# The third of the transposes that put kept V into PSUM goes between scaling and mask of the seventh head

## Chip, cores and metric

The kernel runs on one core of a Trainium2 chip. The metric is the device time of one execution in microseconds (us), the median of several runs. Lower is better.

## The reference, cut to what matters

A decode step for a batch of 4: an attention layer A, a gated layer B, then A and B again with the same weights and the same caches.

```python
W = min(4096, max(256, Sk // 4))                      # 2048 cached positions
k = jnp.repeat(k_cache[:, :, Sk - W:, :], rep, axis=1)   # 8 heads of K/V, 4 query heads each
v = jnp.repeat(v_cache[:, :, Sk - W:, :], rep, axis=1)
scores = jnp.einsum("bhqd,bhkd->bhqk", q, k) * (Dh ** -0.5)
o = jnp.einsum("bhqk,bhkd->bhqd", softmax(scores), v)
A = o.transpose(...).reshape(B, Sq, Hq * Dh) @ wo
B = (sigmoid(x @ w_gate) * (x @ w_up)) @ w_down
x = x + A(layernorm(x)); x = x + B(layernorm(x)); x = x + A(layernorm(x)); x = x + B(layernorm(x))
```

## The kernel before, in words

Attention runs over the 8 heads of K and V one after another, all 4 batches of a head at once. K of all heads stays in SBUF from the first attention to the second (slots 0 to 31 of the tile `arena`); V passes through the remaining slots and is read from memory again for the second attention, except for a few tiles that are kept.

A unit of the first attention (lines 1171 to 1198) is, for head h: transposes of K on VectorE (L854), scores on TensorE (L872, L883), maximum and its spreading on VectorE (L896 to L908), exponentials on ScalarE (L911), a turn of the probabilities (TensorE L924, ScalarE L926, VectorE L931), the sum (TensorE L950) and its reciprocal (VectorE L957), and P times V on TensorE (`pv_unit`, L973, 32 matmuls for each of the two batch pairs). Then come, in this order: the **scaling** of the result by the reciprocal on VectorE (operation `oe0.h`, L981), a small permutation on TensorE (`pm0.h`, L991, 4 matmuls), the **mask** on VectorE (`oq0.h`, L996), and the product with `wo` on TensorE (L1162, 16 matmuls).

Two tiles of V of the last head are kept without staying in their slots. The slots of the tile Y, which is V of head 7 and batch pair 0, are wanted for the weights of the gated layer in between. So Y is moved into PSUM banks 0 to 3 by four VectorE transposes of 128 by 512 words (`stash`, L578, operations `st0` to `st3`), and is moved back in the second attention (L593). Half of the tile Z (batch pair 1) goes into banks 4 and 5 in the same way (`stash_half`, L600, `so0` and `so1`) and comes back at L606.

What sets the order: `_Plan` records operations with their dependences, `_schedule` (L92) makes each engine's order from estimated durations, and `_assign_sync` turns dependences into semaphore waits. Each engine works in its order. The order of the transposes is written out by hand as extra dependences in `attn_first` (lines 1183 to 1195): `st0`, `st1`, scaling of head 6, mask of head 6, `st2`, `st3`, scaling of head 7, `so0`, mask of head 7, `so1`.

All loads go through SyncE's queue in a fixed order (L398). A load waits there until its place in SBUF is free. Around the change these are the places: the fourth piece of `w_gate` goes to the first half of Y (free after `st0`, `st1` and head 7's first P times V), the first piece of `w_up` goes to the second half of Y (free after `st2` and `st3` too), the second piece of `w_up` to Z (free after `so1`), the third and fourth to places that the first pieces of `w_gate` held. The pieces of `w_down` and of `wq` for the second attention follow in the same manner, each into a place that an earlier piece has left.

After `so1` stands the first reduction of the gated layer's layer norm (L745), then its sum on TensorE (L750), the subtraction (L753) and the matmuls with `w_gate` and `w_up` (L1341), one group of four for each piece.

Of the kernel before, what the change touches and what calls it, by code (L numbers as in the profile page):

```python
# [278 lines left out]
def build(nc, A_x, A_k, A_v, A_wq, A_wo, B_wg, B_wu, B_wd, out, cfg=None):  # L279
# [42 lines left out]
    with es:  # L322
# [60 lines left out]
        def tile_ap(s):  # L383
            return arena[:, s * SLOT:(s + 2) * SLOT]
# [4 lines left out]
        def c_dve(n, rate=None):  # L389
            return tm["dve_fix"] + n * (tm["dve_f32"] if rate is None else rate)  # L390
# [65 lines left out]
        def give(*halves):  # L456
            hfree.update(halves)
            fill()

        def need(name):  # L460
            while name not in where:
                take_load()
            return where[name]

        def done(name):
            left[name] -= 1
            if left[name] == 0:
                s = where.pop(name)
                if name in on_free:
                    on_free[name](s)  # L470
                else:
                    pool.release(s)
                fill()
# [99 lines left out]
        def stash(name, ns, after=()):  # L573
            s = need(name)
            for n in ns:
                b = STASH[n]
                src = tile_ap(s)[:, n * 1024:(n + 1) * 1024].bitcast(F32)
                o = P.op("vector", "st%d" % n, c_dve(512), lambda v, src=src, b=b: v.transpose(ps[:, b, :], src),  # L578
                         r=[("slot", s + n // 2)], w=[("stash", n)], banks=(b,), after=after)
            if n == len(STASH) - 1:  # L580
                done(name)
            return o

        def named(name):
            return [o for o in P.ops if o.name == name]
# [12 lines left out]
        def stash_half(n, after):  # L598
            src = slot_ap(base[Z])[:, n * 1024:(n + 1) * 1024].bitcast(F32)
            return P.op("vector", "so%d" % n, c_dve(512), lambda v: v.transpose(ps[:, OBS[n], :], src),  # L600
                        r=[("slot", base[Z])], w=[("so", n)], banks=(OBS[n],), after=after)
# [248 lines left out]
        def k_transpose(h):  # L850
            need(("K", h))
            for t in range(4):
                v32 = slot_ap(4 * h + t).bitcast(F32)
                P.op("vector", "T%d_%d" % (h, t), c_dve(1024), lambda v, v32=v32: v.transpose(v32, v32),  # L854
                     r=[("slot", 4 * h + t)], w=[("slot", 4 * h + t)])
# [66 lines left out]
        def turn_p(L, tag, k2, pb, wide=False):  # L922
            P.op("tensor", "pp" + tag, tm["pe_sq"],
                 lambda pe: pe.matmul(ps[:, pb, :], perm[:, :], prow[:, :], start=True, stop=True),  # L924
                 r=[("prow",)] + perms, w=[("ppb", pb)], banks=(pb,))
            P.op("scalar", "pc" + tag, c_act(512), lambda a: a.copy(prow[:, :], ps[:, pb, :]),  # L926
                 r=[("ppb", pb)], w=[("prow",)], banks=(pb,))
            et = ebuf[:, k2 * 256:(k2 + 1) * 256]
            if wide:
                et = et.rearrange("p (g m x) -> p m g x", g=4, m=8)  # L930
            P.op("vector", "pt" + tag, c_dve(256), lambda v: v.transpose(et, prow[:, :].bitcast(F32)),  # L931
                 r=[("prow",)], w=[("e", k2)])
            if L == 0:
                sums_old(tag, k2)
# [216 lines left out]
        def wo_unit(tag, h, ov, k2, first, final):  # L1151
            name = ("wo", h // 2)
            s = need(name)
            o = h % 2 * REP * D

            half = REP // 2 if tag == "0.%d" % (HKV - 1) else REP
            for r0 in range(0, REP, half):
                def e_wo(pe, r0=r0):
                    last = None
                    for r_ in range(r0, r0 + half):  # L1160
                        for c in range(NC):
                            last = pe.matmul(ps[:, WB, c * NR:(c + 1) * NR],  # L1162
                                             tile_ap(s)[:, o + r_ * D + c * 128:o + r_ * D + (c + 1) * 128],
                                             ov[:, r_ * NR:(r_ + 1) * NR], start=(first and r_ == 0 and c == 0),
                                             stop=(final and r_ == REP - 1), skip_group_check=True)
                    return last
                P.op("tensor", "WO%s_%d_%d" % (tag, h, r0), NC * half * tm["pe_pair"], e_wo,
                     r=[("half",) if r0 else ("slot", s + h % 2)] + [("op", k2)], w=[("psw",)], banks=(WB,))
            done(name)

        def attn_first():
            def front(h):
                k_transpose(h)
                softmax_unit("0.%d" % h, h)
                turn = lambda: turn_p(0, "0.%d" % h, h % 2, PBS[h % 2])
                return turn

            for h in range(2):
                front(h)()
            for h in range(HKV):  # L1180
                tag = "0.%d" % h
                turn = front(h + 2) if h + 2 < HKV else None
                if h == HKV - 1:
                    oe, oq = named("oe0.%d" % (h - 1)), named("oq0.%d" % (h - 1))
                    oe[0].deps.add(stash(stashed, (0, 1)))
                    st = stash(stashed, (2, 3), oq)
                    need(Z)
                op = pv_unit(tag, h, h % 2, v_tiles[(0, h)])
                if h == HKV - 1:
                    oe, oq = named("oe" + tag), named("oq" + tag)  # L1190
                    oe[0].deps.add(st)
                    oq[0].deps.add(stash_half(0, oe))
                    so = stash_half(1, oq)
                    give(base[Z])
                if turn is not None:
                    turn()
                wo_unit(tag, h, op, h % 2, False, h == HKV - 1)
            return so
# [226 lines left out]
        stashed = ("V",) + keep[0] + (0,)  # L1425
# [30 lines left out]
        x_in()  # L1456
        q_first(layer_norm("A", 0, NB, True))
        so = attn_first()
        n = len(P.ops)
        glu(0, 0, NB, (ps[:, WB, 0:REP * NX], [("psw",)], (WB,), lambda: attn_add(0)))  # L1460
# [75 lines left out]
```

## Time and profile before

| | |
|---|---|
| median of 3 runs | 179.22 us (178.72, 179.22, 180.37) |
| the profiled execution | 178.55 us, of which the span from first to last instruction is 176.8 us |
| TensorE busy | 105.5 us (60% of the span), 1653 matmuls |
| VectorE busy | 104.2 us (59%), 256 instructions |
| ScalarE, GpSimd busy | 32.7 us, 21.6 us |
| read from memory | 70.26 MB, 397 GB/s over the span |
| VectorE transposes L578 | 4 instructions, 684 to 728 ns each, from 99.3 us on |
| mean granted clock of TensorE | 0.949 |

Times in the views count from the first instruction. Busy time is the sum of an engine's instructions; "idle before" is the time for which an engine stood before an instruction, with what ended it behind the arrow. The chain of waits is followed back from the last instruction. A line with "x2" covers instructions that follow each other, from the start of the first to the end of the last. SPq is SyncE's queue, which issues the loads; the time to landing of a load runs from its issue to its semaphore.

### The profile page before, as it was taken

How to read it: one execution, taken by the hardware profiler on the slowest of the kernel's cores; microseconds unless marked ns; L12 is line 12 of the kernel's file. 1: busy time of each engine (PE TensorE's matmuls, PEld its weight loads, DVE VectorE, ACT ScalarE, POOL GpSimd, SP SyncE). 2: the span in 40 equal slices, each digit the busy share in tenths (PEclk: the TensorE clock that was granted, in tenths of full speed). 3: DMA queues.
4: the chain of work that ended last, by engine and by line, in shares of the span. 5: the costliest groups of instructions: out<-in, count | busy, mean ns of one | idle time of the engine just before them, and what ended most of it. 6: DMA issues, size and time to landing. Idle time of an engine off the chain costs nothing.

```text
span 176.8 us, 3904 instructions
## 1 busy us (share of the span) xinstructions
PE 105.5 (60%) x1653; PEld 54.7 (31%) x1653; DVE 104.2 (59%) x256; ACT 32.7 (18%) x87; POOL 21.6 (12%) x88
## 2 busy tenths in 40 slices
PE   0536346383852734707518967466877999776754
PEld 0202102241431431603404852052223444345412
DVE  6307997838477375594383582322299999752341
ACT  2002031312030210300301101000043455440011
POOL 6100010101010100100100100000011354342000
PEclk9999999999999999999999999999999999995555
DMA  5999999999999999999999999999999999999991
GB/s 183 426 428 424 423 423 417 411 426 419 417 413 421 423 419 421 411 424 424 411 417 432 400 402 392 406 405 382 410 398 406 423 423 419 419 417 407 405 388 39
DMA packets 12882, 70.52 MB, mean 399 GB/s; under 512 B 1336, under 2 KB 1344, under 8 KB 6720
## 3 DMA queue, kind: packets, MB, share of 16 engines
q1 hardware_dynamic: 12856, 70.26, 97.4%
q8 instruction: 13, 0.21, 0.5%
q14 instruction: 5, 0.04, 0.1%
q10 hardware_dynamic: 8, 0.00, 0.0%
HBM read 70.26 MB, written 0.00 MB: 397 GB/s over the span
## 4 chain that ended last, share of the span: by engine, by line
DMA 38%; DVE 32%; PE 19%; SPq 4%; issue 3%; ACT 2%; DVEq 0%; ACTq 0%
DMA arena<-in_B_w_down_dram 15%; DMA arena<-in_A_v_cache_dram 15%; DVE arena L854 11%; PE ps L883 7%; DVE nmax L896 5%; DMA arena<-in_B_w_gate_dram 4%; DMA arena<-in_A_wq_dram 4%; SPq L398 4%; PE ps L973 3%; PE ps L872 2%; DVE nmax L900 2%; DVE mxt L904 2%; DVE ebuf L931 2%; PE ps L924 2%; DVE arena L1064 2%
## 5 line engine op out<-in xcount | busy, mean ns | idle before, releaser
L854 DVE STREAM_TRANSPOSE arena<-arena 128x1024 f32<-128x1024 f32 x32 | 37.0, 1202 | 0.0
L883 PE MATMUL ps<-arena,qbd 128*32 128x512 bf16 x256 | 25.0, 525 | 0.1
L896 DVE TENSOR_REDUCE nmax<-ps 128x1 f32<-128x512 f32 x16 | 10.8, 676 | 19.6 <-PE ps L883 19.5
L872 PE MATMUL ps<-msk_m,msk_s 128*32 128x512 bf16 x64 | 8.4, 512 | 22.4 <-DVE arena L854 21.8
L973 PE MATMUL ps<-ebuf,arena 128*128 128x8 bf16 x576 | 17.8, 168 | 4.5 <-DMA arena<-in_A_v_cache_dram 4.3
L973 PEld LDWEIGHTS ps<-ebuf,arena 128*128 128x128 bf16 x576 | 16.8, 104 | 9.7 <-DMA arena<-in_A_v_cache_dram 5.3
L911 ACT ACTIVATE prow<-ps,nmax 128x512 bf16<-128x512 f32 x16 | 11.0, 687 | 35.2 <-DVE nmax L908 29.6
L847 ACT CAST qbd<-ps 128x256 bf16<-128x256 f32 x16 | 5.9, 370 | 44.9 <-PE ps L883 35.1
L924 PE MATMUL ps<-prow,perm 128*128 128x512 bf16 x16 | 7.9, 496 | 8.2 <-ACT prow L911 8.2
L940 POOL CAST s<-psm 128x1 bf16<-128x1 f32 x9 | 1.7, 187 | 83.9 <-ACT prow L911 83.9
L883 PEld LDWEIGHTS ps<-arena,qbd 128*32 128x32 bf16 x256 | 8.3, 119 | 10.0 <-issue 7.2
L795 PE MATMUL ps<-arena,xn 128*4 128x512 bf16 x64 | 8.3, 569 | 5.0 <-DMA arena<-in_A_wq_dram 4.7
L926 ACT CAST prow<-ps 128x512 bf16<-128x512 f32 x16 | 9.4, 585 | 9.9 <-PE ps L924 9.9
L1341 PE MATMUL ps<-arena,xn 128*4 128x448 bf16 x64 | 7.6, 550 | 3.8 <-DMA arena<-in_B_w_up_dram 2.1
L931 DVE STREAM_TRANSPOSE ebuf<-prow 128x256 f32<-128x256 f32 x16 | 7.0, 435 | 3.8 <-ACT prow L926 3.7
L872 PEld LDWEIGHTS ps<-msk_m,msk_s 128*32 128x32 bf16 x64 | 1.7, 97 | 24.1 <-DVE arena L854 22.7
L773 ACT ACTIVATE lnv<-ps 128x4 f32<-128x4 f32 x4 | 0.7, 173 | 41.1 <-PE ps L769 41.1
L807 DVE STREAM_TRANSPOSE ebuf<-ps 128x512 f32<-128x512 f32 x3 | 2.2, 717 | 10.2 <-PE ps L795 10.1
L842 PE MATMUL ps<-qh,eyew 32*128 32x64 bf16 x64 | 5.5, 215 | 3.3 <-ACT qbd L847 2.4
L1055 PE MATMUL ps<-arena,ebuf 128*32 128x512 bf16 x112 | 7.3, 381 | 0.2 <-DVE nmax L908 0.2
L1162 PE MATMUL ps<-onp,arena 128*128 128x16 bf16 x144 | 5.3, 175 | 2.9 <-DVE onp L996 2.6
L981 DVE TENSOR_TENSOR onb<-ps,rinv 128x16 bf16<-128x16 f32 x9 | 1.7, 185 | 8.3 <-PE ps L973 8.1
(112 smaller groups left out, 132.6 us busy)
## 6 DMA issues: line engine op xcount, KB each, us to landing
arena<-in_A_v_cache_dram SPq DMA_DIRECT2D x27, 1024.0 KB, 22.4
arena<-in_A_k_cache_dram SPq DMA_DIRECT2D x16, 1024.0 KB, 25.2
arena<-in_A_wq_dram SPq DMA_DIRECT2D x4, 1024.0 KB, 7.9
arena<-in_A_wq_dram SPq DMA_DIRECT2D x8, 512.0 KB, 6.2
arena<-in_A_wo_dram SPq DMA_DIRECT2D x3, 1024.0 KB, 26.2
arena<-in_B_w_down_dram SPq DMA_DIRECT2D x4, 512.0 KB, 6.3
arena<-in_B_w_gate_dram SPq DMA_DIRECT2D x4, 448.0 KB, 8.2
arena<-in_B_w_up_dram SPq DMA_DIRECT2D x4, 448.0 KB, 5.4
```

Source lines behind the costliest of these rows:

```text
L795: last = pe.matmul(ps[32 * hh:32 * hh + NB, qb, :], xn[:, c * NB:(c + 1) * NB], src[:, o + hh * 512:o + (hh + 1) * 512], start=(c == 0), s ...
L854: P.op("vector", "T%d_%d" % (h, t), c_dve(1024), lambda v, v32=v32: v.transpose(v32, v32), r=[("slot", 4 * h + t)], w=[("slot", 4 * h + t)])
L872: last = pe.matmul(ps[32 * gi:32 * gi + 32, bank, :], msk_s[:, :], msk_m[:, :].unsqueeze(1).broadcast_to([128, 256, 2]), start=True, stop= ...
L883: last = pe.matmul(ps[32 * gi:32 * gi + 32, bank, :], qbd[:, q0:q0 + 32], kt[:, cp // 2, cp % 2, jh * NJ:(jh + 1) * NJ, :], start=False, s ...
L896: lambda v: v.tensor_reduce(nmax[:, k2:k2 + 1], ps[:, bank, :], AXX, ALU.max),
L911: lambda a: a.activation(prow[:, :].rearrange("p (m x t) -> p m x t", x=32, t=2), ps[:, bank, :].rearrange("p (m t x) -> p m x t", x=32, t ...
L924: lambda pe: pe.matmul(ps[:, pb, :], perm[:, :], prow[:, :], start=True, stop=True),
L926: P.op("scalar", "pc" + tag, c_act(512), lambda a: a.copy(prow[:, :], ps[:, pb, :]), r=[("ppb", pb)], w=[("prow",)], banks=(pb,))
L931: P.op("vector", "pt" + tag, c_dve(256), lambda v: v.transpose(et, prow[:, :].bitcast(F32)), r=[("prow",)], w=[("e", k2)])
L973: last = pe.matmul(ps[:, ob, bp * 8:bp * 8 + 8], src[:, j * 128:(j + 1) * 128], ev[:, j % 2, j % 16 // 2, x0:x0 + 8], start=(j == 0), stop ...
L1055: last = pe.matmul(ps[32 * g:32 * g + 32, ob, :], ew[:, g, mq, t], src.rearrange("p (m t d) -> p t m d", t=2, d=128)[:, t], start=(n == 0) ...
L1341: last = pe.matmul(ps[32 * g:32 * g + NB, gub[n], 0:NF], xn[:, c * NB:(c + 1) * NB], slot_ap(s)[:, g * NF:(g + 1) * NF], start=(c == 0), s ...
```

## The change

`st2` and `st3` were recorded together, both after the mask of head 6 (`oq0.6`). Now `st2` depends on the scaling of head 6 (`oe0.6`), the mask depends on `st2`, and `st3` depends on the mask. VectorE's order becomes: `st0`, `st1`, scaling, `st2`, mask, `st3`, scaling of head 7. No instruction is added or removed, and the orders of TensorE, ScalarE, GpSimd and SyncE's queue are those of before. The mask waits for two semaphores now (VectorE's own, for `st2`, and TensorE's).

```diff
                 if h == HKV - 1:
                     oe, oq = named("oe0.%d" % (h - 1)), named("oq0.%d" % (h - 1))
                     oe[0].deps.add(stash(stashed, (0, 1)))
-                    st = stash(stashed, (2, 3), oq)
+                    oq[0].deps.add(stash(stashed, (2,), oe))
+                    st = stash(stashed, (3,), oq)
                     need(Z)
```

## Prediction

> **What bounds the kernel now.** I read the page first (engine shares, slices, queues), then the chain of waits from 97 us on, then VectorE's and TensorE's timelines around the transposes, then the loads' times to landing, and last the stretches of the gated layer.
>
> The page, slices and queues:
>
> ```profile
> span 176.8 us, 3904 instructions
> PEclk9999999999999999999999999999999999995555
> DMA  5999999999999999999999999999999999999991
> q1 hardware_dynamic: 12856, 70.26, 97.4%
> HBM read 70.26 MB, written 0.00 MB: 397 GB/s over the span
> ```
>
> No compute engine is above 60%, but the 16 DMA engines are 90% busy or more in every slice but the first and the last; queue 1 alone takes 97.4% of their time. Only a change that lets the stream of loads begin earlier, run dry less, or end with a shorter tail moves the end. The last load lands at 173.35 us (chain: 152.41 + 20.94), and the tail behind it takes 3.4 us.
>
> The chain of waits, its long pieces of the stretch after the change:
>
> ```profile
> 101.75 7.12 DMA arena<-in_B_w_gate_dram
> ...
> 110.89 6.29 DMA arena<-in_B_w_down_dram
> ...
> 117.85 6.48 DMA arena<-in_A_wq_dram
> ...
> 152.41 20.94 DMA arena<-in_B_w_down_dram
> ```
>
> From 101.75 us on the chain is a line of loads that stand in the queue behind other loads. 448 KB at 405 GB/s are 1.13 us of transfer, so most of the 7.12 us of the first is waiting for its turn.
>
> VectorE's timeline, start, length, instruction:
>
> ```profile
> 99.30 1.32 DVE L578 STREAM_TRANSPOSE ps<-arena 128x512 f32<-128x512 f32 x2
> 100.73 0.20 DVE L981 TENSOR_TENSOR onb<-ps,rinv 128x16 bf16<-128x16 f32 x1
> 101.87 0.23 DVE L996 TENSOR_TENSOR onp<-ps,maskp 128x64 bf16<-128x64 f32 x1 [0.95 <-PE ps L991]
> 102.13 1.32 DVE L578 STREAM_TRANSPOSE ps<-arena 128x512 f32<-128x512 f32 x2
> 103.55 0.19 DVE L981 TENSOR_TENSOR onb<-ps,rinv 128x16 bf16<-128x16 f32 x1
> 103.78 0.73 DVE L600 STREAM_TRANSPOSE ps<-arena 128x512 f32<-128x512 f32 x1
> 104.61 0.23 DVE L996 TENSOR_TENSOR onp<-ps,maskp 128x64 bf16<-128x64 f32 x1
> ```
>
> Between scaling and mask of the seventh head VectorE stands for 0.95 us, until the permutation on TensorE ends. The third and fourth transposes follow the mask.
>
> TensorE's timeline in the same stretch:
>
> ```profile
> 101.58 0.25 PE L991 MATMUL ps<-onb,permo 128*128 128x16 bf16 x4
> 101.83 1.02 PE L973 MATMUL ps<-ebuf,arena 128*128 128x8 bf16 x32
> 103.11 0.59 PE L1162 MATMUL ps<-onp,arena 128*128 128x16 bf16 x16 [0.27 <-DMA arena<-in_A_wo_dram]
> 103.80 0.28 PE L991 MATMUL ps<-onb,permo 128*128 128x16 bf16 x4
> 104.98 0.58 PE L1162 MATMUL ps<-onp,arena 128*128 128x16 bf16 x16 [0.90 <-DVE onp L996]
> ```
>
> The permutation starts only at 101.58 because 32 matmuls of head 7 (L973) stand ahead of it, though the scaling was done at 100.93. What the mask feeds, the product with `wo` of head 6, starts at 103.11: its load ended the wait, not the mask, which was done at 102.10.
>
> **The change part by part.**
>
> *The transpose goes into the hole.* `st2` waits for the scaling, done at 100.93 (100.73 + 0.20); the next instruction after such a wait starts some 0.04 later (scaling ends 103.74, `so0` starts 103.78). A single transpose that is waited for takes 0.73 (L600 row). So `st2` runs from 100.96 to 101.69.
>
> *The mask behind it.* It now also waits for `st2`; from the end of a transpose to the mask that waits for it the row shows 0.10 (104.51 to 104.61), so it could start at 101.79. The permutation ends at 101.83 and the mask started at 101.87. The mask stays at 101.87: cost nothing, cover 0.08 us. If that cover is gone the mask is late by what is missing, but the `wo` product behind it waits for its load until 103.11, 1.0 us after the mask's end; even a mask behind a whole 0.73 would be hidden there. Nothing else waits for the mask; on VectorE only `st3` stands behind it.
>
> *What becomes earlier.* `st3` alone after the mask: 102.13 to 102.85, where the pair ended at 103.45. The scaling of head 7 needs `st3` and the second 32 matmuls, which end at 102.85 too; at 102.95 it can start, against 103.55. That is 0.6 us, not the 0.73 of a transpose: the two back to back took 1.32 and not 1.46, and this overlap goes. A rule of the Trainium skill speaks here, "VectorE: DVE Perf Modes", section "The DRAIN you can't avoid": the next VectorE instruction starts only when the pipe is empty, and a semaphore between two costs nothing extra. By it the moved transpose would save its whole 0.73. The pair's 1.32 us does not agree, and the measurement is used.
>
> Then: `so0` 103.18 to 103.91; the permutation of head 7 follows the `wo` product of head 6 at about 103.70 (it was 103.80) and ends by 104.0; the mask of head 7 at 104.02 (was 104.61), held by `so0`; `so1` ends at 105.00 (was 105.60); the last `wo` products start at about 104.4 instead of 104.98, and their last loads, issued at 96.5 with 7.9 us to landing, are there at 104.4. The layer norm's first reduction starts at 105.10 instead of 105.70, and the first `w_gate` matmul at about 106.33 instead of 106.92. So 0.6 us is gained up to that matmul.
>
> *Where that stops.* The pieces of `w_gate` land at about 105.5, 106.6, 107.8 and 108.9 (issues 97.0, 97.4, 99.8, 101.75 with 8.5, 9.2, 8.0, 7.1 us to landing). The third group of matmuls waits for its load at 107.8 already now, so from there TensorE is back at the old times. What is late next is the load, and 0.6 us of compute falls away.
>
> *The queue.* Every load keeps its place. The first piece of `w_up` waits in SyncE's queue for `st3`: issued at 103.47, after the change at about 102.88. The second waits for `so1`: 105.67, then about 105.08. The third and fourth wait for the first two groups of `w_gate` matmuls (107.51 and 107.88), up to 0.6 earlier. `w_down` behind them waits for the third group and stays at 108.37. They are issued earlier into a queue that is busy: the second lands at 105.67 + 5.4 = 111.1, the one ahead of it at 103.47 + 6.5 = 110.0. An earlier issue brings an earlier landing only where the engines had too little in the queue. The stretches say where:
>
> ```profile
> 107.00:109.00 2.00, 1.42 (x16) 0.20 (x15) 0.24 (x2) 0.00 (x0) 0.00 (x0) 1.00 1.03 405
> 109.00:110.50 1.50, 1.17 (x10) 0.62 (x8) 0.69 (x2) 0.45 (x3) 0.00 (x0) 1.00 0.99 363
> 110.50:112.00 1.50, 0.89 (x8) 0.09 (x4) 0.89 (x3) 0.27 (x2) 0.00 (x0) 1.00 1.05 401
> 122.50:124.00 1.50, 0.60 (x4) 0.09 (x4) 0.22 (x1) 0.00 (x0) 0.00 (x0) 1.00 0.94 320
> ```
>
> The last two columns are the share of the DMA engines and GB/s. In 109.0 to 110.5 the stream moved 363 GB/s against 401 just after: (401 - 363) / 401 x 1.5 = 0.14 us lost at most to a thin queue. Whether that was a thin queue or slow packets (share 0.99) no row shows, so the gain lies between 0 and 0.14. A loss at this place is excluded, as no load is issued later. I take 0.1 us. The larger hole at 122.5 (320 against 415 GB/s later, 0.34 us) hangs on the fifth `wq` piece, whose place comes free after the second layer norm; that starts with the last `w_down` landing at 117.85, so the hole moves with the stream and stays.
>
> *The end.* After 130 us loads stand 8 to 22 us in the queue, the tail is untouched, and whatever the stream gained at 110 arrives at the end.
>
> Sum: hole filled -0.6 on VectorE, hidden behind the landing of `w_gate`; mask 0; queue -0.1 (0 to -0.14). The span goes from 176.8 to 176.7, the profiled execution from 178.55 (1.7 us around the span) to 178.45. That execution lies 0.67 below the median 179.22 and 0.17 below the lowest of the three runs. I forecast for the median 179.1.
>
> **The rivals.**
>
> 1. *The 0.6 us goes through.* If the stream after 103 us is in truth a closed loop, in which each load waits for a place and each place for an earlier load, then the 0.6 us by which the `w_up` issues advance moves everything behind them. For it: the chain goes issue, load, matmul, issue from 101.75 to 124 us. Against it: the engines' share stays at 0.99 to 1.05. Time: 179.2 - 0.6 = 178.6, still within 1%.
>
> 2. *The mask is late.* If the permutation ends sooner than now or `st2` runs longer than 0.81, the mask waits for it. Worst case: mask held for a whole transpose, 0.73. From 1.0 us of lateness on, the `wo` product on TensorE would be late; below that nothing is. So even this gives 179.2. If also the overlap of transposes cost more than 0.1 at each break, at most one more 0.73, the end of `so1` would be 0.1 late instead of 0.6 early: 179.3.
>
> 3. *The slower side: TensorE's clock falls earlier.* The granted clock is 1.00 until the stretch 155 to 160 us (0.87) and 0.50 from there; with half of the clock from about 158.7 us. What sets the moment no row shows. TensorE is busy 4.37, 5.00, 5.00, 3.98 us in the 5 us stretches from 135 to 155. At half the clock these 18.4 us would take up to 18.4 more, and places for the loads come free later. Cover: the first large `w_down` load of the end is issued at 151.9 and lands 20.2 later, while 4.7 us was enough for the third `w_up` piece, so 15.5 us are hidden. With 2.8 us more for the busy part of 155 to 158.7 (3.68 x 0.75), an onset at 135 would cost 21.2 - 15.5 = 5.7 us: 185. It decides where 15.5 us of TensorE's work lie behind the onset, which is at about 141 us, and passes 1% (1.8 us more) at about 139. Against it: the change shifts one VectorE instruction, and TensorE's instructions, order and, after 107.8 us, times are the same.
>
> 4. *The change does not do what it says.* Excluded for the order, which the new dependences fix; the hole of 0.95 us is in one profiled execution and rests on 32 matmuls ahead of the permutation, so it is there in each.
>
> **How the numbers follow.** Forecast (gain 0 to 0.14): 0.74. Rival 1, 178.6: 0.12. Rival 2, 179.2 to 179.3: 0.05. Rival 3, above 181: 0.05. The remaining 0.04 is for a median that strays by over 1% to the fast side. The three runs span 178.72 to 180.37, 0.9%; about 1% is what a measurement of this kernel can tell from no change. Forecast and rivals 1 and 2 are within 1%: 0.91, of which I give 0.01 to slower for a stray median: faster 0.04, same 0.90, slower 0.06. The range: low is rival 1 on the lower of the forecast's runs, 178.72 - 0.6 = 178.1; high is the highest run shown, 180.4, as the forecast leaves this spread as it is.
>
> **What would show each step.** `st2` at about 100.96, mask still at 101.87, no hole on VectorE above 0.2 us there; `st3` ending at 102.85; the scaling of head 7 at 102.95; layer norm's reduction at 105.1; issues of the first two `w_up` pieces at 102.9 and 105.1, with times to landing longer by 0.5 us (7.0 and 5.9). If these times to landing stay at 6.5 and 5.4 instead, rival 1 holds. If the mask starts after 101.9, rival 2. If the granted clock falls before 141 us, rival 3. The prediction is wrong if the last landing moves by more than 0.2 us against the span's start.

## The result, and the profile after

| | before | after |
|---|---|---|
| median of 22 runs of each, on the same chips | 179.41 us (178.31 to 181.34) | 178.61 us (178.44 to 179.28) |
| runs above 179.3 us | 12 of 22 | 0 of 22 |
| the profiled execution, its span | 178.55, 176.8 us | 178.86, 177.1 us |

The ratio of the times is 0.9955 [0.9936, 0.9975]: 0.8 us or 0.45% faster, less than the 1% and more than the 0.1 us that I had taken. The fastest executions of the two kernels are equal; what the change takes away are the longer ones. (179.3 us as a mark was set once the runs were known: just above the longest of the changed kernel.) Ratios and their intervals, here and below, leave out runs more than 1.5% above the fastest of their kernel and need not be the quotient of the two medians. The two profiled executions do not show the gain: that of before was one of its fastest, that of after lies 0.25 above its own median.

The page of the changed kernel, the same rows as for before:

```profile
span 177.1 us, 3893 instructions
PEclk9999999999999999999999999999999999975555
DMA  5999999999999999999999999999999999999980
q1 hardware_dynamic: 12856, 70.26, 97.2%
HBM read 70.26 MB, written 0.00 MB: 397 GB/s over the span
```

Same bound, nearly the same share of queue 1. The clock falls a little earlier in this execution: a mean of 0.73 in 155 to 160 us against 0.87, which is 1.4 us (0.14 of 5 us at a step of 0.5). That is far behind the 141 us from which rival 3 had it matter.

VectorE's timeline of the changed kernel, start, length, instruction:

```profile
99.45 1.32 DVE L578 STREAM_TRANSPOSE ps<-arena 128x512 f32<-128x512 f32 x2 [0.27 <-DMA arena<-in_A_v_cache_dram]
100.87 0.19 DVE L981 TENSOR_TENSOR onb<-ps,rinv 128x16 bf16<-128x16 f32 x1
101.10 0.73 DVE L578 STREAM_TRANSPOSE ps<-arena 128x512 f32<-128x512 f32 x1
101.93 0.23 DVE L996 TENSOR_TENSOR onp<-ps,maskp 128x64 bf16<-128x64 f32 x1
102.19 0.73 DVE L578 STREAM_TRANSPOSE ps<-arena 128x512 f32<-128x512 f32 x1
103.02 0.20 DVE L981 TENSOR_TENSOR onb<-ps,rinv 128x16 bf16<-128x16 f32 x1
...
104.34 0.73 DVE L600 STREAM_TRANSPOSE ps<-arena 128x512 f32<-128x512 f32 x1
105.17 0.23 DVE L745 TENSOR_REDUCE lnr<-ps 128x4 f32<-128x64 f32 x1
```

Of before, the row that this one is compared with:

```profile
105.70 0.23 DVE L745 TENSOR_REDUCE lnr<-ps 128x4 f32<-128x64 f32 x1
```

The hole of 0.95 us is gone, and each instruction stands within 0.07 us of its predicted place, except `st2` (101.10, predicted 100.96), as `st0` itself waited for a load of V 0.15 us longer in this execution. The reduction starts at 105.17; predicted was 105.10, and before it was 105.70.

TensorE and SyncE's queue in the changed kernel, two views:

```profile
101.58 0.25 PE L991 MATMUL ps<-onb,permo 128*128 128x16 bf16 x4
...
103.25 0.59 PE L1162 MATMUL ps<-onp,arena 128*128 128x16 bf16 x16 [0.27 <-DMA arena<-in_A_wo_dram]
...
106.39 0.99 PE L1342 MATMUL ps<-arena,xn 128*4 128x448 bf16 x8 [0.36 <-DVE xT L757]
107.94 0.54 PE L1342 MATMUL ps<-arena,xn 128*4 128x448 bf16 x4 [0.56 <-DMA arena<-in_B_w_gate_dram]
```

```profile
101.75 0.33 SPq L398 DMA_DIRECT2D arena<-in_B_w_gate_dram  x1
102.95 4.84 SPq L398 DMA_DIRECT2D arena<-in_B_w_up_dram  x4
108.53 0.33 SPq L398 DMA_DIRECT2D arena<-in_B_w_down_dram  x1
```

And in the kernel before:

```profile
106.92 1.41 PE L1341 MATMUL ps<-arena,xn 128*4 128x448 bf16 x12 [0.36 <-DVE xT L757]
```

```profile
103.47 4.84 SPq L398 DMA_DIRECT2D arena<-in_B_w_up_dram  x4
108.37 0.41 SPq L398 DMA_DIRECT2D arena<-in_B_w_down_dram  x1
```

The permutation and `st2` both end at 101.83 and the mask starts 0.10 later; the cover of 0.08 us was used up to the last. The `wo` product behind it still waits for its load. The first `w_gate` matmul comes at 106.39 (106.92), the third group waits for its load until 107.94, and from there the gain of the compute is gone: `w_down` is issued at 108.53, 0.16 later than before, as the load of the third group landed 0.16 later too (107.90 against 107.74). The four `w_up` loads were issued at 102.95, 105.14, 106.98 and 107.43; before it was 103.47, 105.67, 107.51 and 107.88.

The chain of the changed kernel has the same long pieces:

```profile
101.75 7.31 DMA arena<-in_B_w_gate_dram
...
111.08 6.26 DMA arena<-in_B_w_down_dram
...
118.01 6.33 DMA arena<-in_A_wq_dram
...
152.83 20.84 DMA arena<-in_B_w_down_dram
```

The stretches, changed kernel, with the share of the DMA engines and GB/s last:

```profile
109.00:110.50 1.50, 1.07 (x9) 0.63 (x10) 0.65 (x1) 0.27 (x2) 0.00 (x0) 1.00 1.03 409
110.50:112.00 1.50, 1.08 (x8) 0.17 (x8) 0.94 (x3) 0.45 (x3) 0.00 (x0) 1.00 1.01 380
122.50:124.00 1.50, 0.60 (x4) 0.09 (x4) 0.21 (x1) 0.00 (x0) 0.00 (x0) 1.00 1.03 341
```

The 363 GB/s at 109.0 have become 409, the 401 behind them 380: at this place the change is worth about the 0.1 us of the forecast.

**The landings.** A load ends with 16 increments of its semaphore. From the trace, the time of the last one, in us:

```
load                               before   after    difference
V, 12 us before the moved transpose  89.33    89.48    +0.15
4th w_gate                         108.87   109.06    +0.19
1st wq                             119.13   119.28    +0.15
2nd wq                             120.69   120.55    -0.14
8th wq                             128.41   128.15    -0.26
first whole V load of 2nd attention 135.61  134.52    -1.09
the next                           138.28   138.22    -0.06
four later                         148.15   148.55    +0.40
the last large w_down              173.36   173.67    +0.31
```

So against its own start the changed kernel gains 0.3 us, and not where `w_up` lands but between the first and the second `wq` load, some 10 us later; at the first V loads of the second attention most of it is lost again, and the rest of the difference comes about far behind the change. Two single executions tell nothing of 0.8 us between medians. That needed more runs. What they do show is the bound: in all 14 traces of this document the execution ends 4.4 to 4.7 us after the last of its loads has landed, whether it took 178.21 or 182.86 us.

### The profile page after: what moved, and what is told of

Read it like the earlier page. It is cut to its first block, busy times and chain, and to the rows that moved or that the text cites. A ratio compares the mean times of both kernels' runs of the same rounds, so it can differ in the third digit from the quotient of the medians.

```text
span 177.1 us, 3893 instructions
## 1 busy us (share of the span) xinstructions
PE 102.2 (58%) x1641; PEld 55.0 (31%) x1653; DVE 104.4 (59%) x256; ACT 32.7 (18%) x87; POOL 21.6 (12%) x88
## 4 chain that ended last, share of the span: by engine, by line
DMA 38%; DVE 32%; PE 18%; issue 4%; SPq 4%; ACT 3%; DVEq 0%; ACTq 0%
DMA arena<-in_B_w_down_dram 15%; DMA arena<-in_A_v_cache_dram 15%; DVE arena L854 11%; PE ps L883 7%; DVE nmax L896 5%; DMA arena<-in_B_w_gate_dram 4%; DMA arena<-in_A_wq_dram 4%; SPq L398 4%; PE ps L973 3%; PE ps L872 2%; DVE nmax L900 2%; DVE mxt L904 2%; DVE ebuf L931 2%; PE ps L1162 2%; DVE arena L1064 2%
## 5 line engine op out<-in xcount | busy, mean ns | idle before, releaser
L883 PE MATMUL ps<-arena,qbd 128*32 128x512 bf16 x256 | 25.5, 534 | 0.0
L1055 PE MATMUL ps<-arena,ebuf 128*32 128x512 bf16 x112 | 8.0, 409 | 0.2 <-DVE nmax L908 0.2
L1351 DVE STREAM_TRANSPOSE ebuf<-ps 128x448 f32<-128x448 f32 x4 | 2.6, 650 | 7.0 <-PE ps L1342 7.0
```

What stands on the lines that cost most here:

```text
L883: last = pe.matmul(ps[32 * gi:32 * gi + 32, bank, :], qbd[:, q0:q0 + 32], kt[:, cp // 2, cp % 2, jh * NJ:(jh + 1) * NJ, :], start=False, s ...
L1055: last = pe.matmul(ps[32 * g:32 * g + 32, ob, :], ew[:, g, mq, t], src.rearrange("p (m t d) -> p t m d", t=2, d=128)[:, t], start=(n == 0) ...
```

## The experiments

Four theories were put to the test. **A**: the loss of before varies from execution to execution, at a place where the queue is thin; an earlier issue takes the bad ones away. **B** (rival 1): the 0.6 us go through to the end, the same in each execution. **C**: the 16 DMA engines are not in step; the ones that finish their share of a load first have a head start over the last, and a late issue uses it up, which costs nothing until the next disturbance. **D**: only the first two `w_up` loads count, those that the change advances directly. C and D were set up after the first four experiments.

Each kernel's time stands beside runs of the kernel before on the same chip: 179.39 (35 runs) for the first four, 179.37 (34) for the next four, 179.04 (17) for the last four. Where an instruction is repeated, it writes the same values again.

**1. The kernel before, again**, with no edit.

> The kernel before once more, to see its single executions: they lay between 178.31 and 181.34 us, those with the change between 178.44 and 179.28. Theory A (a loss that varies: in some executions the stream of loads runs dry in the gated layer because w_up is issued late, in others not): median about 179.4, executions spread over some 2 us, and an execution above 180 shows a hole in the loads that a fast one lacks. Theory B (a fixed 0.6 us of compute that goes through to the end): the executions lie together and the ratio is 1.000; the spread shown so far came from different chips.

Measured: 179.73 us (178.95 to 181.82, 12 runs), ratio 0.9995 [0.9958, 1.0033]; 7 of 12 above 179.3. The spread is that of before.

**2. The changed kernel, again**, with no edit.

> The changed kernel on the same chip as the runs beside it. Theory A: ratio about 0.995, its executions within 0.8 us of each other while those of before spread over 2 us; the fastest executions of both are equal within 0.2 us. Theory B: ratio 0.9965, and the fastest execution is also 0.6 us below the fastest of before.

Measured: 178.67 us (178.55 to 179.27, 12 runs), ratio 0.9949 [0.992, 0.9979]; 0 of 12 above 179.3. Together with the first comparison 34 executions of the changed kernel, none above 179.3. The gain is real, and A's narrow spread is there. B, with a fixed gain, has nothing for equal fastest executions.

**3. Before, with `st2` done twice**: the three transposes take 2.08 us where two took 1.32, and the scaling of head 7 and the `w_up` issues come 0.66 us later still.

```diff
+        TWICE = 2
...
-            for n in ns:
+            for n in [m for m in ns for _ in range(2 if m == TWICE else 1)]:
```

> The kernel before with the third transpose done twice (same result, 0.63 us more on VectorE), so that the fourth transpose, the scaling of head 7, so0, so1 and the issues of the first two w_up loads come 0.6 us later still: 104.1 and 106.3. Theory A: the queue is thinner by another 0.6 us, the loss comes in more executions or is larger: median 179.8 to 181. Theory B: 0.6 us more, 180.0, with the same spread as before. The forecast on record (hidden, queue at most 0.14): 179.5, ratio within 1.001.

Measured: 180.26 us (179.43 to 181.07, 12 runs), ratio 1.0046 [1.001, 1.0082]; all 12 above 179.3. A's range holds it, and by the time alone B (180.0) is not excluded; here the fastest execution is later too, by 0.95 us. The forecast on record, 179.5, is missed. Its VectorE timeline:

```profile
101.77 0.23 DVE L997 TENSOR_TENSOR onp<-ps,maskp 128x64 bf16<-128x64 f32 x1 [0.83 <-PE ps L992]
102.03 2.08 DVE L579 STREAM_TRANSPOSE ps<-arena 128x512 f32<-128x512 f32 x3
104.21 0.19 DVE L982 TENSOR_TENSOR onb<-ps,rinv 128x16 bf16<-128x16 f32 x1
```

`w_up` is issued at 104.13, 106.33, 108.17 and 108.55. Two stretches of it:

```profile
109.00:110.50 1.50, 1.17 (x10) 0.65 (x10) 0.66 (x2) 0.42 (x3) 0.00 (x0) 1.00 0.93 332
118.50:120.00 1.50, 0.93 (x6) 0.62 (x6) 1.37 (x7) 0.00 (x0) 0.00 (x0) 1.00 0.97 325
```

The same second stretch of the changed kernel, and of the kernel before:

```profile
118.50:120.00 1.50, 0.73 (x6) 0.62 (x6) 1.38 (x6) 0.00 (x0) 0.00 (x0) 1.00 1.02 404
118.50:120.00 1.50, 0.89 (x6) 0.62 (x6) 1.35 (x7) 0.00 (x0) 0.00 (x0) 1.00 1.01 396
```

There are two holes, one where the queue is thin (332) and one 9 us later (325), where the loads had been issued some 7 us before they landed. In the traced execution of before, one of its fastest, the second stretch is hardly thinner (396) than with the change (404). The second hole is where most of the time goes: the last landing of the fourth `w_up` is as early as before (113.30 against 113.33), of the first `wq` too (119.08 against 119.13), but the second `wq` lands at 121.22 against 120.69, 0.53 us late.

**4. The changed kernel, with `st3` done twice**: its order, but the loads are issued as in the kernel before (103.57, 105.77, 107.60, 107.98).

```diff
+        TWICE = 3
...
-            for n in ns:
+            for n in [m for m in ns for _ in range(2 if m == TWICE else 1)]:
```

> The changed kernel with the fourth transpose done twice, which takes back the 0.6 us: the fourth transpose ends at 103.5, layer norm and the first two w_up issues are where they were before the change, while the third transpose stays between scaling and mask. Theories A and B: as before, ratio 0.999 to 1.001, for A with the spread of before. If the place of the third transpose itself matters and not the time it saves, it is as fast as the changed kernel, 0.9955.

Measured: 180.19 us (178.37 to 180.98, 12 runs), ratio 1.0014 [0.9974, 1.0054]; 10 of 12 above 179.3. The gain is gone: it hangs on what comes earlier behind the transposes, and not on the order as such.

**5. The changed kernel, with the norm's first reduction done three times**: the first two `w_up` loads as early as with the change, the third and fourth later by 0.5 us against the first, as the place they go to is freed later.

```diff
-            P.op("vector", "ln_red" + tag, ds,
...
+            for _ in range(3 if tag == "G0" else 1):
+                P.op("vector", "ln_red" + tag, ds,
```

> The changed kernel with the first reduction of the gated layer's norm done three times (same result, 0.5 us more on VectorE): the third transpose stays in the hole and the first two w_up loads stay early (102.9 and 105.1), but the norm, the first two groups of w_gate matmuls and with them the issues of the third and fourth w_up load are back where they were before the change (107.5 and 107.9). Theory C (the loss is head start: the engines that are ahead run dry behind the second w_up load because the third is issued late, and the next fetch of instructions on one engine is then seen at the last landing): as before, ratio 0.998 to 1.002, landings of a load spread over 1.5 us instead of 1.9 by the first w_down load. Theory D (the early issue of the first two w_up loads is what counts): as fast as the changed kernel, 0.995. Theory B (any 0.6 us goes through): as before.

Measured: 178.74 us (178.21 to 180.56, 12 runs), ratio 0.9971 [0.9936, 1.0007]; 3 of 12 above 179.3. Between the two kernels, and its interval reaches both C's 0.998 and D's 0.995: it decides nothing.

**6. The changed kernel, with the first two `w_up` loads held back** (issues 103.82, 105.37, 106.79, 107.21).

```diff
+        named(str(("wu", 0, 0)))[0].deps.add(named("so0")[0])
+        named(str(("wu", 1, 0)))[0].deps.add(named("xr0")[0])
```

> The changed kernel with the first two w_up loads held until after so0 and after the reduction into x, so that they are issued at 104.0 and 105.6, as late as before the change or later, while the norm and the third and fourth w_up load stay early. Theory C: as fast as the changed kernel, 0.995, narrow spread, landings still 1.9 us apart at the first w_down load. Theory D: as before, 1.000. Theory B: 0.995.

Measured: 179.01 us (178.53 to 180.99, 12 runs), ratio 0.9987 [0.9948, 1.0025]; 5 of 12 above 179.3. Between again; C had a narrow spread here, and 178.53 to 180.99 is not narrow.

**7. Before, with `so0` behind the mask of head 7 and `so1` behind the norm's first reduction**: the norm earlier without the change (issues 103.36, 106.28, 107.01, 107.38).

```diff
-                    oq[0].deps.add(stash_half(0, oe))
-                    so = stash_half(1, oq)
+                    so = stash_half(0, oq)
+                    z1 = stash_half(1, oq)
...
+        z1.deps.add(named("xr0")[0])
```

> The kernel before, third and fourth transpose behind the mask as they were, but so0 goes behind the mask of head 7 and so1 behind the norm's first reduction: the norm starts at about 105.2 as with the change, the first w_up load is issued at 103.5 as before and the second at about 106.2, later than before. Theory C: the third w_up load is issued at about 107.0, so as fast as the changed kernel, 0.995, narrow spread, though the change is not in it. Theory D: as before or slower, 1.000 to 1.003. Theory B: 0.9965.

Measured: 178.97 us (178.53 to 180.9, 12 runs), ratio 0.9995 [0.9956, 1.0034]; 4 of 12 above 179.3. C had 0.995 and a narrow spread, and misses both. Whether early third and fourth loads bring a part of the gain here, and keep a part of it in 6, is not shown by intervals as wide as these.

**8. Before, with `st2` done three times** (issues 104.98, 107.18, 109.02, 109.39).

```diff
-            for n in ns:
+            for n in [m for m in ns for _ in range(3 if m == 2 else 1)]:
```

> The kernel before with the third transpose done three times: everything behind it 1.27 us later, the third w_up load issued at 108.8. Theory C: the head start of the engines falls to 0.5 us or less at the third w_up load, the last landing itself may be late by 0.3 us there, and the next fetch of instructions (1.05 us on one engine) is seen nearly whole: median 180.3 to 181, fastest execution above 179.4. Theory B: 1.27 us more than before, 180.7, same spread. The forecast on record (hidden): 179.5.

Measured: 181.82 us (180.75 to 183.07, 11 runs), ratio 1.0126 [1.0085, 1.0166]; the issues are 1.51 us later than in before. It is slower than both C (180.3 to 181) and B (180.7) had it, and the fastest execution is later by 2.35 us. Now the hole is open at once:

```profile
110.00:111.00 1.00, 0.67 (x10) 0.59 (x6) 0.65 (x1) 0.32 (x3) 0.00 (x0) 1.00 0.91 158
```

158 GB/s in this microsecond; the third `w_up` lands 3.02 us behind the second instead of 1.12. The engines' share is 0.91 all the same: from 106 to 112 us the trace has 34 packets of 0.3 to 1.15 us among 527, against 0.14 in a full queue. The share of busy time hides such a hole, the GB/s show it.

**9. The changed kernel, with the norm's first reduction nine times**: only the third and fourth `w_up` loads late (102.84, 105.04, 108.94, 109.32).

```diff
-            P.op("vector", "ln_red" + tag, ds,
...
+            for _ in range(9 if tag == "G0" else 1):
+                P.op("vector", "ln_red" + tag, ds,
```

> The changed kernel with the first reduction of the gated layer's norm done nine times (same result, 2 us more on VectorE): the first two w_up loads stay early (102.9, 105.1), the third and fourth are issued at about 108.9 and 109.3, later than in any kernel but the one with the third transpose done three times. Theory C (head start of the DMA engines, used up behind the second w_up load): slow in nearly every execution, median above 180.3. Theory D (the first two w_up loads count): as the changed kernel, 178.7. If neither place alone matters, about 179.4.

Measured: 181.48 us (180.32 to 182.28, 6 runs), ratio 1.0113 [1.0055, 1.0171]. Its VectorE timeline and a stretch:

```profile
105.06 2.29 DVE L746 TENSOR_REDUCE lnr<-ps 128x4 f32<-128x64 f32 x9
```

```profile
109.00:110.50 1.50, 1.50 (x14) 0.64 (x6) 0.43 (x1) 0.00 (x0) 0.00 (x0) 1.00 0.75 237
```

The third `w_up` lands 2.20 us behind the second instead of 1.12, the second `wq` 2.18 behind the first. D is out as it stood: with the first two loads early, the kernel is 2.4 us slower than before, though `w_down` behind them is late as well (109.79 against 108.37).

**10. The changed kernel, with only the first two `w_up` loads much later** (105.06, 106.95, 107.32, 107.80; the last two are earlier than in before).

```diff
+        named(str(("wu", 0, 0)))[0].deps.add(named("so1")[0])
+        named(str(("wu", 1, 0)))[0].deps.add(named("glwg0_0")[0])
```

> The changed kernel with the first two w_up loads held until so1 and until the first group of w_gate matmuls is done: issued at about 105.1 and 107.0, 2 us later than with the change, while the norm stays early; the third and fourth follow at once (107.3, 107.6). Theory C: the queue is refilled before the engines in front reach its end at the third load, so at most a part of the loss: median 178.7 to 179.2. Theory D: as slow as with the third transpose done three times, above 180.3.

Measured: 180.82 us (179.73 to 181.91, 12 runs), ratio 1.0077 [1.004, 1.0115]. A miss for C as I had put it, with the third and fourth loads alone at fault (178.7 to 179.2); D, which 9 put out, had this one right:

```profile
107.00:109.00 2.00, 0.90 (x8) 0.09 (x4) 0.00 (x0) 0.00 (x0) 0.00 (x0) 1.00 0.99 344
```

The queue is thin at 107 here, and no `w_up` landing is late at all (1.08 to 1.15 us apart), but the second `wq` lands 2.34 us behind the first. With 9, this speaks against either pair of loads as the only cause, and for the depth of the queue behind `w_gate`.

**What happens at the second `wq`.** The trace holds 13 packets of 16,384 bytes on the queue that the page calls "instruction", in the kernel before one for each 174 to 331 recorded instructions of TensorE, 257 on average (3,348 in 13). There each takes 1.02 to 1.11 us. What one does is seen where the queue is deep: up to the first of them, at 30.88 us, the 16 landings of a load lie within 0.28 us; at the twelfth load, the next to land, 15 still lie within 0.28 and one is 1.45 us behind them, and it stays behind. So a packet holds up one of the 16 engines. In 11 and 12 below, where the first packet comes at 24.5, one landing is 1.2 us behind the other 15 at the ninth load already. One of the packets comes at about 118.5. The spread of a load is the time from its first to its last of 16 landings, the head start of the foremost engine. For comparison, the fourth `w_gate` has a spread of 1.8 to 2.3 us in all kernels. From the traces:

```
kernel                        spread at    2nd wq lands   the 16 KB packet
                              1st wq, us   after 1st, us  between, at us
changed                       1.87         1.27           118.32
changed, again (2)            1.84         1.25           119.13
7 (so1 later)                 1.83         1.26           118.43
6 (loads held)                1.85         1.66           118.62
5 (norm three times)          1.71         1.26           118.55
before, again (1)             1.50         1.82           118.89
4 (changed, st3 twice)        1.47         1.95           118.80
before                        1.46         1.55           118.54
9 (norm nine times)           1.21         2.18           119.80
10 (loads much later)         1.14         2.34           118.96
3 (before, st2 twice)         1.02         2.14           118.59
12 (changed, packets moved)   1.67         1.28           none
11 (before, packets moved)    2.03         1.27           none
8 (before, st2 three times)   1.81         1.28           119.91
```

Where the spread has shrunk to 1.5 us or less, the second `wq` is late by 0.3 to 1.1 us (gap less 1.27, the transfer alone). Where it is still 1.7 us or more, it is on time in all kernels but 6 (0.4 late); in 2 and 5 the third `wq` comes 0.5 and 0.25 us late instead. Kernel 8 had its hole before and came out of it with a new spread. Where the second `wq` is late it is again one landing: in 10 and in 3 it comes 1.08 and 0.63 us behind the other 15. This one place does not explain the whole time: 2 has no hole here and its traced execution took 179.06 us, before has one of 0.3 and took 178.55.

The Trainium skill ("Runtime: NRT & Kernel Launch", section "Instruction fetch mechanics") says that an engine's instructions are fetched in blocks of 16 KiB, 256 instructions, over a DMA queue of its own, at a cost that is mostly hidden. Size and number agree with this case's trace. Hidden it is not where a load lands late by it, as the second `wq` does here by 0.3 to 1.1 us, if the packet is the cause; the landings and the moved places in 11 and 12 speak for it.

**11. Before, with 80 more small matmuls** (the spreading of q in heads 2 to 6, five times): the 16 KB packets should move away from 118.5.

```diff
-                for a in range(4):
+                for a in list(range(4)) * (5 if tag in ("0.2", "0.3", "0.4", "0.5", "0.6") else 1):
```

> The kernel before with 80 matmuls done again in the heads 2 to 6 (the spread of q, same result, in time in which TensorE waits for VectorE), which puts TensorE's instructions 160 further on. If the 16 KB packets on queue 8 are fetches of TensorE's instructions, 256 at a time, the one at 118.5 us comes at about 108, before the queue is thin, and the one at 134 at about 125. Theory C: the hole in the landings of the second wq load is gone (1.27 us behind the first, where before shows 1.56), executions nearer to each other: median 178.4 to 179.0, faster than before without the change. Theory B (0.6 us of compute goes through): ratio 1.000. If the fetch at 125 falls into the second thin place, the hole moves there and the median stays at 179.4; the place of the hole tells.

Measured: 181.7 us (180.19 to 184.11, 6 runs), ratio 1.0132 [1.0063, 1.02]. The time was missed. The packets moved to 102.14, 109.36 and 123.11; the second `wq` lands 1.27 us behind the first, as expected, but the third `w_up`, which lands after the packet at 109.36, now comes 2.40 us behind the second. And the matmuls were not free, VectorE's timeline shows:

```profile
105.14 0.22 DVE L996 TENSOR_TENSOR onp<-ps,maskp 128x64 bf16<-128x64 f32 x1 [0.71 <-PE ps L991]
105.40 0.73 DVE L600 STREAM_TRANSPOSE ps<-arena 128x512 f32<-128x512 f32 x1
106.23 0.23 DVE L745 TENSOR_REDUCE lnr<-ps 128x4 f32<-128x64 f32 x1
```

The mask of head 7 waits for TensorE, and the norm is 0.5 us later than before. At the V loads of the second attention it is the same: in all kernels but this one and the next a packet at 133.5 to 136.4 us goes with a first or second whole V load that comes late (the two take 5.7 to 6.4 us together), here the packet comes at 139.01, these two take 4.97, and the third comes 3.28 us behind the second instead of 2.5. The place of the hole follows the packet; its price can't be read from this kernel.

**12. The changed kernel, with the same 80 matmuls.**

```diff
-                for a in range(4):
+                for a in list(range(4)) * (5 if tag in ("0.2", "0.3", "0.4", "0.5", "0.6") else 1):
```

> The changed kernel with the same 80 matmuls done again. Theory C: no hole at the second wq load in either, so the two differ less than the change does by itself: median within 0.3 us of the run beside it. Theory B: 0.6 us below the run beside it.

Measured: 181.47 us (180.52 to 182.53, 6 runs), ratio 1.0109 [1.005, 1.0168]. Within 0.3 us of 11, as C had it; but the mask of head 7 waits here as well (105.26), the norm is as late as in 11, and the change advances only the first `w_up` issue (103.08 against 103.40). So this does not tell C from B. The packets are at 102.27, 109.28, 123.38 and 140.54; the holes are at the third `w_up` (1.97 us behind the second), the fourth `wq` (3.12 instead of 1.28) and the third whole V load (3.74 instead of 2.5).

## Why the prediction was right, and where its size failed

- *The bound.* Right: the end follows the last landing in each trace (4.4 to 4.7 us behind it), and each kernel whose loads are issued clearly later (3, 8, 9, 10, and 4 against 2) is slower, with no compute engine above 60%. One reading was off: the load that lands at 173.35 is not the last. A smaller piece of `w_down`, issued at 159.03, lands at 173.99, and the tail behind it is 2.8 us.
- *`st2` in the hole, mask at no cost.* Right: the mask was 0.06 us later (101.93 against 101.87), within what waits for a load behind it.
- *The 0.6 us.* Right: the reduction came 0.53 us earlier, 0.07 less than forecast; counted from the mask, which was 0.06 later, it is 0.59. That the pair's overlap is lost was read rightly: 0.73 us for each of the two now, with 0.10 to the instruction that waits, where the pair had 1.32. I had quoted the Trainium skill ("VectorE: DVE Perf Modes", "The DRAIN you can't avoid") against this row; the same section also says that a next instruction that is not held starts earlier, which the pair does. It does not disagree; I had read half of it.
- *Absorbed at 107.8.* Right: third group at 107.94, behind its load.
- *The issues.* Right: 102.95 and 105.14 (102.9 and 105.1), `w_down` 0.16 later, with the landing that it hangs on. The times to landing are 7.2 and 6.15 us (7.0 and 5.9).
- *The queue, 0 to 0.14 us, 0.1 taken.* **This is the term that was mis-sized**, with 0.8 us between the medians, 1.1 in experiment 2 against experiment 1 (179.73 and 178.67). I read the bound from one stretch of one execution, and that execution was among the fastest of before, one in which the thin queue cost little. And I looked for the loss only in the stretch in which the queue is thin. What the runs showed in its place: executions of before lie above 179.3 us in about half of the cases (66 of 120 over all comparisons), those of the changed kernel never (0 of 34). And in the traces an issue that is 0.5 us later goes with a smaller head start of the engines in front and with a loss up to 10 us behind (second `wq`: 0.3 to 0.7 us late in before, 1 and 4, on time in the changed kernel). That this loss is what makes the slower half of before slower is not shown: none of these executions was traced.
- *The range.* 178.1 to 180.4 held the result by its width: its lower end came from rival 1, its upper end from the spread of before. The forecast itself, 179.1, lay 0.5 us above.
- *Rival 1.* Its number, 178.6, was nearer than mine, in part by chance: it was taken from the median of three runs, 179.22, and from 179.41 it would have been 178.8. Its mechanism was not there: the times to landing grew, the fastest executions of the two kernels are equal, so it is not a fixed 0.6 us.
- *Behind 130 us loads stand deep enough.* Too strong. The first whole V load of the second attention, issued at 128.24, has only 7.4 us to landing. It and the next should take 5.0 us together and take 6.06 in before, 6.23 in after, each with a 16 KB packet at 134. This is where the two profiled executions come level again (-1.09, then -0.06).
- *"Wrong if the last landing moves by more than 0.2 us".* It moved by 0.31, to the later side. By my own mark the prediction falls; but 0.15 of it was there at 89 us, before the change, and landings of single executions differ by more than this mark. It was set without a look at the spread.

What is shown: the gain comes from what is earlier behind the transposes (4 takes it back; 3 and 8, with later issues, are slower still), it is variable (34 executions against those of before), and a thin queue behind `w_gate` costs in both ways tried, in 10 through the issues of two loads alone. That a packet sets one engine back is shown by the landings, in every trace and at the moved places in 11 and 12. That the gain comes about through head starts and these packets is argued, from the landings of one execution per kernel; 6 and 7 do not fit by their times, 2 and 5 only in part, it was not turned on and off by itself, and no execution of before above 179.2 us was traced. Open are: what the first two and the last two `w_up` loads count for at small delays (5, 6 and 7 lie between the kernels, with overlapping intervals); which of the 16 engines a packet meets, which the landings do not tell; and the gap behind the fifth `wq` load, which was not tried (the load that comes late there is the sixth, issued at 120.34, not the fifth as the prediction had it). No version beat the changed kernel.

## What to carry to other kernels

When a stream of loads is the bound, the issue that comes last into a thin queue is a place of loss even if its landing looks early enough: read GB/s and not the busy share, and follow the loss to later loads, not only to that stretch. A single profiled execution bounds nothing that varies between executions: look at the spread of the runs shown (178.72 to 180.37 here) and ask what makes it. A reorder on an engine that is off the bound can be worth its spread alone.

## What the runs showed of the hardware that was not expected

- The 16 DMA engines of one load are not in step: in before, first and last landing are 0.28 us apart at the tenth load, 1.73 at the twelfth (34.49), with the first 16 KB packet at 30.88 between them, and stay some 1.7 to 1.9 apart as long as the queue is deep. At first it is one landing that lags.
- One 16 KB packet takes 1.02 to 1.11 us in before, 13 times in an execution; in the thin queue at 109.3 us it took 1.95 (11) and 1.48 (12).
- Where the stream thins out, some packets of 3,584 bytes take 0.3 to 1.15 us, against 0.14 in a full queue (kernel 8, 106 to 112 us), and the page's share of busy time counts them as busy (0.91 at 158 GB/s).
- Being late costs more than itself: between medians, 0.66 us later cost 0.9 us (3) and 1.51 us later 2.4 us (8), the latter at one load 1.9 us at once, and 0.52 us earlier gained 0.8. That is 1.3 to 1.6 us for each us in all three; that it grows is not shown.
